# A gated mix of two sequence layers on one core: one load moved to another queue, three groups of work reordered

## The chip, the core and the metric

The kernel runs on one core of a Trainium2 chip. That core has a matrix engine (PE, with PEld for its weight loads), a vector engine (DVE), an engine for activations and scaling (ACT), a general engine (POOL) and SyncE (SP), which only issues DMAs here. DMAs are issued from the queues of SP, ACT and POOL. Every engine works through its own instruction list in order; engines wait for one another by semaphores. The metric is the device time of one execution in microseconds (us), lower is better; "ns" marks nanoseconds.

## The reference

The inputs are x, k and v (2048 x 1024, bfloat16), a diagonal state-space layer A (1024 complex states, matrices B and C, step sizes, a skip vector) and a long convolution B (a 4-tap shift kernel, an ssm kernel of length 2048 per channel, a skip vector).

```python
g = sigmoid((x * gate_w).sum(-1, keepdims=True))
# A: h[t] = Lam_bar * h[t-1] + B_bar x[t];  y = 2 Re(C h) + x * Dskip
a = A_ref(x, Lambda_re, Lambda_im, B_re, B_im, C_re, C_im, log_dt, Dskip)
# B: kv = (4-tap shift of k) * v;  y = fft-convolution of kv with ssm_k over the sequence, + kv * ssm_D;  x * y
b = B_ref(x, k, v, shift_k, ssm_k, ssm_D)
out = g * a + (1 - g) * b
```

## The kernel before

The kernel is one long program in which the order on every engine is written out by hand: the helper `put` chains each instruction behind the one before it on its engine, so PE, DVE, ACT, POOL and SP do their work in the order in which the code emits it. Nearly every instruction therefore has line 94 in the profile, and the tiles tell them apart.

**Opening (lines 147 to 353 and 1022 to 1063).** ACT's queue loads the small parameters: `B_shift_k` (into `skr`), `gate_w` (into `gwr`), then three rows of state parameters (`prow`), and later `B_ssm_D` (`sD`). SP's queue loads the first chunk of 128 channels: two halves of k by DMA transpose (`kT0`), the first half of v between them (`v0`), the ssm kernel by transpose (`kn`), then v's second half. PE starts with dummy products (`raise_clock`), makes columns out of the parameter rows with small products into the PSUM tile `psp` (`columns` does the later ones), and runs the 4-tap sums (`taps`) for both halves. DVE multiplies each half of the taps by v (`ks`). `state_params` (the generator `sp`) has small steps on ACT and DVE: `dtv`, then `abv` on DVE and `rv` on ACT, then more. `fold_K` folds the ssm kernel with ten products into two PSUM tiles (`foldk`), which ACT copies out (`eok`); `mirror` and two DVE sums do the same for v; `fwd_K` and `fwd_V` are the transforms (`psk`, `psv`).

**Convolution loop (lines 1075 to 1195).** For the eight chunks of channels: forward transforms on PE, the complex products of the two spectra on DVE (`products`, tiles G, BT, wkh, t), the inverse transform on PE (`inverse`, PSUM `psz`, copied by ACT to `cv` and stored by SP). Products with x for layer A (`Bu`, PSUM `odd`, `even`, `both`) fill PE in between, with the tiles in `order`, numbered 0 to 15.

**Passage (lines 1197 to 1292).** The last chunk's products and the tiles `Bu(6)`, `Bu(7)`, and the first half of `Bu(8)`. From tile 4 on, the tiles are finished by `turn_U`: ACT scales U's odd half into Q, and POOL adds Q to U's even half by an accumulating DMA, twice, one step after the other; the second addition waits until the first has landed. The 2 by 8 tiles of C are turned by the parameters in `turn_C` (`turning[0]` to `turning[7]`): ACT scales into `m` (or `Q` for pairs 4 and 5), then ACT or DVE scales C itself, and the sum is made by POOL's accumulating DMAs (pairs 0, 1, 4, 5) or on DVE (pairs 2, 3, 6, 7). Tile `u4` has three buffers: U6, the Q of tile 6, and U7 take them, and U8 takes the one that tile 6's Q gives back. PSUM has four buffers for everything.

**Scan loop (lines 1369 to 1419).** Sixteen steps j: DVE scans one state tile (`scan`), `turning` and `turn_U` of later tiles run where the step says so, and `plan[j]` names the products of PE: B8 is tile 8, C0 is the first row block of the output's product with C (PSUM `psy`), G10 a group. `on_act` holds steps of `turn_C` that ACT takes one by one between the copies of `Bu_next` (`filler`). After the loop the last four blocks are finished and stored.

Of the kernel before, what the change touches and what calls it, by code (L numbers as in the profile page):

```python
# [11 lines left out]
BF16 = mybir.dt.bfloat16  # L12
# [8 lines left out]
def kernel(  # L21
# [26 lines left out]
    nc = tc.nc  # L48
    xf = A_x.flatten_outer_dims()
    kf = B_k.flatten_outer_dims()  # L50
    vf = B_v.flatten_outer_dims()
    of = out.flatten_outer_dims()
    S, D = xf.shape
    P = A_Lambda_re.shape[0]
    KS = B_shift_k.shape[1]
    assert S == 2048 and D == 1024 and P == 1024, (S, D, P)
    ND = D // 128
    NP = P // 128
    NT = S // 128
# [6 lines left out]
    PAD = 16  # L66
# [13 lines left out]
    s5p = {"wu": pool("wu", 3)}  # L80
# [11 lines left out]
    def put(eng, f, *a, **kw):  # L92
        with tc.issue_after(prev[eng]) if eng in prev else nullcontext():
            i = f(*a, **kw)  # L94
        prev[eng] = getattr(i, "ins", i)

    def mm(o, l, r, first, last):
        put("pe", nc.tensor.matmul, o, lhsT=l, rhs=r, start=first, stop=last)
# [15 lines left out]
    def copy(o, a):  # L114
        put("dve", V.tensor_copy, o, a)
# [7 lines left out]
    def move(o, i):  # L123
        put("sp", nc.sync.dma_start, out=o, in_=i)
# [17 lines left out]
    ld = pool("ld", 3, side="right")  # L142
# [11 lines left out]
    gwr = rows_[32:32 + ND, 128 * KS:128 * KS + 128]  # L154
    prow = rows_[64:64 + 3 * ND, 0:128]

    nc.scalar.dma_start(out=skr, in_=B_shift_k.rearrange("(j p) k -> j p k", p=128))
    nc.scalar.dma_start(out=gwr, in_=gate_w.rearrange("(j p) -> j p", p=128))
    for i, ap in enumerate((A_log_dt, A_Lambda_re, A_Lambda_im)):
        nc.scalar.dma_start(out=prow[i * ND:(i + 1) * ND, :], in_=ap.rearrange("(j p) -> j p", p=128))  # L160
    pih = consts.tile([128, 1], F32, name="pih")
# [3 lines left out]

    one = consts.tile([128, 1], F32, name="one")
    put("act", nc.scalar.activation, out=one, in_=pih, func=ACT.Sin)
    nc.scalar.dma_start(out=sD, in_=B_ssm_D.rearrange("(o d) -> o d", o=1))

    lds = {}  # L170

# [3 lines left out]
    def load(which, c, held=False):  # L175
        cc = slice(c * 128, (c + 1) * 128)
        if which == "kn":

            t = ld.tile([128, NT, 128], BF16, name="kn", tag="ld")
            if held:  # L180
                hold(t[:, 0, 0:1])
            load_t(t, B_ssm_k[cc, :])
        elif which == "v":

            w = 2 if c == 2 else 1
            if c == NC - 1:
                t = ld.tile([128, NT, 128], BF16, name="v", tag="ld")
            elif c == 2:
                lds["v2"] = xt_pool.tile([128, NT, 2, 128], BF16, name="v2", tag="xT")
            if c < 2:  # L190
                t = ld.tile([128, NT, 128], BF16, name="v", tag="ld")
            elif c < NC - 1:
                t = lds["v2"][:, :, c % 2:c % 2 + w].rearrange("p n k d -> p n (k d)")
            if held:
                hold(t[:, 0, 0:1])
            move(t, vf.rearrange("(n p) d -> p n d", p=128)[:, :, c * 128:(c + w) * 128])
            for k in range(w):
                lds["v", c + k] = t[:, :, k * 128:(k + 1) * 128]
            return
        else:  # L200

            t = ld.tile([128, PAD + S], BF16, name="kT", tag="ld")
            put("pool", nc.gpsimd.memset, t[:, 0:PAD], 0.0)
            if held:
                hold(t[:, PAD:PAD + 1])
            load_t(t[:, PAD:], kf[:, cc])
            if c >= 3:
                lds["kB", c] = ld.tile([128, PAD + S], BF16, name="kB", tag="ld")
        lds[which, c] = t
# [8 lines left out]
        move(a[hi, 10:], a[lo, 8:n - 2])  # L218


    kT0 = ld.tile([128, PAD + S], BF16, name="kT", tag="ld")
    v0 = ld.tile([128, NT, 128], BF16, name="v", tag="ld")
    put("pool", nc.gpsimd.memset, kT0[:, 0:PAD], 0.0)
    for h in range(2):
        hs, ns = slice(h * S // 2, (h + 1) * S // 2), slice(h * NT // 2, (h + 1) * NT // 2)
        load_t(kT0[:, PAD + hs.start:PAD + hs.stop], kf[hs, 0:128])
        if h == 1:
            load("kn", 0)
        move(v0[:, ns], vf.rearrange("(n p) d -> p n d", p=128)[:, ns, 0:128])
    lds["kT", 0], lds["v", 0] = kT0, v0  # L230

    BT = [bt_pool.tile([128, 2, ND, 256], BF16, name=f"BT{g}") for g in range(NG)]
# [52 lines left out]
    ident = consts.tile([128, 128], BF16, name="ident")  # L285
# [3 lines left out]
    def raise_clock(n):  # L289
        for _ in range(n):  # L290
            mm(raised[:, 0], zeros[:, 0:128], zeros, True, True)
# [13 lines left out]
    gwb = consts.tile([128, ND], BF16, name="gwb")  # L305
    pcol2 = consts.tile([128, 4, ND], F32, name="pcol2")
    ident2 = consts.tile([128, 64], BF16, name="ident2")
    psp = ps2([128, 2, 512], "p")
# [7 lines left out]
    dg0 = ks_pool.tile([128, KS, 128], BF16, name="dg", bufs=1)  # L316
    for k in range(KS):
        ts(dg0[:, k], ident, pcol[:, 3 + k, 0:1], None, ALU.mult)
    raise_clock(2)
    mm(psp[:, 1, KS * ND:(KS + 1) * ND], gwr, ident[32:32 + ND, 32:32 + ND], True, True)  # L320
    raise_clock(1)

    def columns():
        mm(psp[:, 0, 0:3 * ND], prow, ident[64:64 + 3 * ND, 64:64 + 3 * ND], True, True)
        copy(pcol[:, 0:3], psp[:, 0, 0:3 * ND].rearrange("p (i j) -> p i j", j=ND))
        copy(gwb, psp[:, 1, KS * ND:(KS + 1) * ND])
        yield
        for q in range(4):
            for t in range(2):
                mm(psp[t * 64:t * 64 + 64, 1, 64 + q * ND:64 + (q + 1) * ND],  # L330
                   skr[:, q // 2 * 64:q // 2 * 64 + 64, q % 2 + 2 * t], ident[32:32 + ND, 32:32 + ND], True, True)
        copy(pcol2, psp[:, 1, 64:64 + 4 * ND].rearrange("p (i j) -> p i j", j=ND))
        tt(ident2, ident[:, 0:64], ident[:, 64:128], ALU.add)

# [464 lines left out]
    turns_U = {}  # L799
# [210 lines left out]
    def step(gen):  # L1010
        next(gen, None)

    def run(gen):
        for _ in gen:
            pass

    def steps(gen, n):
        for _ in range(n):
            step(gen)
# [11 lines left out]
    sp = state_params()  # L1031
# [2 lines left out]
    inverse_cols()  # L1034
    ts(NCF, CF, -1.0, None, ALU.mult)
    step(first)
    step(sp)
    angles = inverse_angles()
    turns = inverse_table()
    run(columns)  # L1040
    run(fold_K(0))
    step(angles)
    run(first)
    dg1 = dgs(1, True)
# [30 lines left out]
    for c in range(NC - 1):  # L1075
        n, nn = c + 1, c + 2
# [157 lines left out]
    with tc.tile_pool(name="fin", bufs=1, side="right") as fin:  # L1234

        count = iter(range(16))

        def room(shape, dt, name):
            return fin.tile(shape, dt, name=name, tag=f"fin{next(count)}")

        prod, back = products(c, 0, room, False), inverse(c - 1)
        run(old)
        steps(prod, 3)
        run(next(tiles))
        steps(turning[0], 2)
        step(back)
        steps(turning[1], 2)
        run(back)
        gate(1)
        gate(2)  # L1250
        steps(prod, 2)
        b6, b7 = Bu(6)
        run(b6)
        run(b7)
        run(turning[0])
        s5p["Q"] = s5p["wu"]
        step(turns_U[6])
        run(turning[1])
        run(prod)
        run(turns_U[6])  # L1260
        b8, b9 = Bu(7)
        run(b8)
        run(b9)
        load_xT(3)
        b10, b11 = Bu(8)
        run(b10)
    back = inverse(c)
    step(back)
    run(back)
    steps(turning[2], 2)  # L1270
    h3.close()
    wk = pool("wk", 5)
    s5p["hb"] = pool("hb", 7)
# [18 lines left out]
    on_act = []  # L1292
# [77 lines left out]
    for j in range(NS):  # L1370
        for k in loaded.get(j, ()):
            loads(k)
        if j == 7:
            store(3)
        for k in stored.get(j, ()):
            store(k)
        advance(j)
        for t in turning[2 * j:2 * j + 2]:
            run(t)
        if j == 0:  # L1380
            run(turning[2])
        on_act += [lambda t=t: step(t) for t in turning[max(3, 2 * j + 2):2 * j + 4] for _ in range(2)]
        turn = turns_U[turned[j]] if j in turned else none
        if j != 10 and plan[j][0:1] != "G":
            step(turn)
        by_group = plan[j][0:1] == "G" and j != 10
        if j == 7:
            scale_b(6)
        if by_group:
            for n, k in enumerate(scaled_b.get(j, ())):  # L1390
                if n == 1:
                    step(turn)
                scale_b(k)
            run(turn)
        if j == 4:
            put_off[-1][0]()
            scale_b(3)
        for unit in plan[j].split():
            if unit == "C0":
                scale_b(2)  # L1400
            if unit[0] == "G":
                Cy_group(int(unit[1]), int(unit[2]))
            else:
                (Bu_next if unit[0] == "B" else Cy_row)(int(unit[1:]), *([[b11]] if unit == "B8" else []))
        if put_off and j not in (4, 12):
            put_off[-1][0]()
        if j == 10:
            step(turn)
            for k in scaled_b[j]:
                scale_b(k)  # L1410
            run(turn)
        elif not by_group:
            run(turn)
            if j == 5:
                run(turns_U[5])
            for k in scaled_b.get(j, ()):
                scale_b(k)
        if j == 7:
            gate(3)
# [48 lines left out]
```

## Time and profile before

| | |
|---|---|
| median of 3 runs | 388.67 us (388.26 to 390.49) |
| the profiled execution: time, span in the trace | 389.03 us, 387.3 us |
| busy in the span: PE, DVE, ACT, POOL | 97%, 96%, 76%, 20% |
| mean DMA rate | 183 GB/s |

A row of a timeline has the start and the length in us, then engine, line, operation, output tile <- input tiles, shapes and a count; in brackets stands how long the engine was idle just before and what released it. In the chain of work that ended last a row is a start, a length and what the chain ran through; "issue" there is time in which the engine waited for nothing that the profile shows. "SPq", "ACTq" and "POOLq" are DMA issues. A row of the view by stretches has, for each engine, its busy us and its number of instructions, then the granted PE clock (1.00 is full), the busy share of the core's DMA engines and their rate. A row of a DMA issue ends with the bytes of one and the median us from issue to landing.

### The profile page before, as it was taken

How to read it: one execution, taken by the hardware profiler on the slowest of the kernel's cores; microseconds unless marked ns; L12 is line 12 of the kernel's file. 1: busy time of each engine (PE TensorE's matmuls, PEld its weight loads, DVE VectorE, ACT ScalarE, POOL GpSimd, SP SyncE). 2: the span in 40 equal slices, each digit the busy share in tenths (PEclk: the TensorE clock that was granted, in tenths of full speed). 3: DMA queues.
4: the chain of work that ended last, by engine and by line, in shares of the span. 5: the costliest groups of instructions: out<-in, count | busy, mean ns of one | idle time of the engine just before them, and what ended most of it. 6: DMA issues, size and time to landing. Idle time of an engine off the chain costs nothing.

```text
span 387.3 us, 6616 instructions
## 1 busy us (share of the span) xinstructions
PE 376.0 (97%) x2445; PEld 196.8 (51%) x2445; DVE 371.5 (96%) x602; ACT 293.8 (76%) x448; POOL 77.5 (20%) x101
## 2 busy tenths in 40 slices
PE   8899899999999999999999899999999999999995
PEld 5466347565484756754454344444444444444442
DVE  8789999999999999999999969999999999999996
ACT  5799997988979789774769398985998859947601
POOL 4011030110301102030004000323323333635100
PEclk9999999999999999999999999999999999999999
DMA  8959999999999998967698989995899999898902
GB/s 158 171 113 234 193 214 191 220 218 155 218 207 215 212 192 173 182 146 137 121 209 174 176 188 213 212 202 102 150 212 212 198 244 239 147 251 160 235 3 108
DMA packets 135506, 70.72 MB, mean 183 GB/s; under 512 B 114921, under 2 KB 117745, under 8 KB 135474
## 3 DMA queue, kind: packets, MB, share of 16 engines
q1 hardware_dynamic: 122992, 46.16, 56.1%
q0 software_dynamic: 12400, 24.12, 37.3%
q8 instruction: 19, 0.31, 0.3%
q14 instruction: 13, 0.11, 0.1%
q10 hardware_dynamic: 82, 0.02, 0.0%
HBM read 12.86 MB, written 8.39 MB: 55 GB/s over the span
## 4 chain that ended last, share of the span: by engine, by line
PE 59%; DVE 20%; ACT 7%; DMA 6%; issue 4%; SPq 2%; DVEq 0%; ACTq 0%
PE psy L94 29%; PE psk L94 7%; DVE BT L94 5%; PE both L94 5%; DVE wkh L94 4%; PE psz L94 4%; PE psv L94 3%; PE even L94 3%; PE taps L94 3%; PE odd L94 3%; DVE G L94 2%; PE foldk L94 2%; SPq L94 2%; DMA U<-Q 2%; DMA CT<-Q 1%
## 5 line engine op out<-in xcount | busy, mean ns | idle before, releaser
L94 PEld LDWEIGHTS <-BT 128*128 128x128 bf16 x640 | 61.7, 98 | 50.5 <-issue 1.7
L94 PE MATMUL both<-xT,BT 128*128 128x512 bf16 x384 | 84.0, 379 | 1.8 <-ACT U L94 1.4
L94 PEld LDWEIGHTS <-hb 128*128 128x128 bf16 x256 | 25.0, 98 | 30.9 <-issue 1.1
L94 PEld LDWEIGHTS <-U 128*128 128x128 bf16 x240 | 23.5, 98 | 28.3
L94 PE MATMUL psy<-CT,hb 128*128 128x512 bf16 x160 | 36.8, 379 | 0.0
L94 ACT ACTIVATE Vh<-psv 128x1024 bf16<-128x1024 f32 x32 | 30.8, 1035 | 7.7 <-PE psv L94 7.6
L94 POOL DMA_DIRECT2D U<-Q x22 | 23.3, 1072 | 62.8 <-ACT Q L94 25.4
L94 PE MATMUL psy<-CT,U 128*128 128x512 bf16 x152 | 34.8, 379 | 0.0
L94 ACT ACTIVATE U<-both 128x512 bf16<-128x512 f32 x44 | 24.2, 594 | 13.9 <-PE both L94 13.7
L94 DVE TENSOR_TENSOR_SCAN W<-rv,init,A 128x256 bf16<-128x256 f32 x48 | 32.1, 729 | 0.0
L94 POOL DMA_DIRECT2D G<-wkh x8 | 9.7, 1218 | 102.8 <-DVE wkh L94 102.8
L94 PE MATMUL psk<-eok,SF 128*128 128x512 bf16 (+1 forms) x120 | 28.1, 354 | 0.0
L94 PEld LDWEIGHTS <-SF 128*128 128x128 bf16 x184 | 18.0, 98 | 19.8 <-issue 1.3
L94 ACT ACTIVATE Q<-U,lam 128x512 bf16<-128x512 bf16 (+1 forms) x44 | 25.5, 606 | 1.1 <-DMA CT<-Q 1.1
L94 PE MATMUL psz<-G,CI 128*128 128x512 bf16 x64 | 24.3, 380 | 1.3 <-DVE G L94 1.3
L94 PE MATMUL psz<-G,SI 128*128 128x512 bf16 x64 | 24.3, 379 | 0.0
L94 PE MATMUL psy<-CTa,hb 128*128 128x512 bf16 x96 | 22.7, 379 | 0.6 <-ACT U L94 0.6
L94 PE MATMUL taps<-dg,kT 128*128 128x128 bf16 (+1 forms) x352 | 21.7, 209 | 0.4 <-DMA kT<-in_B_k_dram 0.4
L94 DVE TENSOR_TENSOR wkh<-BT,Vh 128x3072 bf16<-128x3072 bf16 (+4 forms) x20 | 21.8, 1109 | 0.0
L94 PEld LDWEIGHTS <-kT 128*128 128x128 bf16 x352 | 21.2, 100 | 1.2 <-DMA kT<-in_B_k_dram 0.5
L94 DVE TENSOR_TENSOR wkh<-Kh,Vh 128x3072 bf16<-128x3072 bf16 (+2 forms) x16 | 21.3, 1349 | 0.0
L94 PE MATMUL psk<-eok,CF 128*128 128x512 bf16 x64 | 19.3, 379 | 1.3 <-ACT eok L94 1.3
(221 smaller groups left out, 841.8 us busy)
## 6 DMA issues: line engine op xcount, KB each, us to landing
U<-Q POOLq DMA_DIRECT2D x22, 256.0 KB, 5.2
G<-wkh POOLq DMA_DIRECT2D x6, 768.0 KB, 8.7
cv_scr<-cv SPq DMA_DIRECT2D x16, 256.0 KB, 4.1
v<-in_B_v_dram SPq DMA_DIRECT2D x5, 512.0 KB, 5.7
out_dram<-m SPq DMA_DIRECT2D x8, 256.0 KB, 6.7
BT<-cv_scr SPq DMA_DIRECT2D x7, 256.0 KB, 5.9
out_dram<-BT SPq DMA_DIRECT2D x7, 256.0 KB, 3.5
ks<-lo POOLq DMA_DIRECT2D x6, 256.0 KB, 8.3
```

The costliest lines, as they stand in the source:

```text
L94: i = f(*a, **kw)
```

## The change

Four things move; no product, sum or byte is added or removed.

1. v's first chunk goes from SP's queue to ACT's queue: its first half right behind `B_shift_k`, its second half behind the activation `one`. SP's queue then has k, k, `kn` back to back.
2. `gate_w`'s load goes to the end of ACT's opening loads, its product on PE from the dummy products into the second step of `columns`, and its copy (`gwb`) with it. That second step of `columns` now comes ahead of `fold_K(0)` as before, but the step of `state_params` with `abv` and `rv` comes behind `fold_K(0)`.
3. In the passage, both steps of `turn_U` for tile 6 come ahead of the second parts of `turning[0]` and `turning[1]`.
4. `turning[2]` (C's third tile) is no longer half done before the scan loop and finished in step 0; it is handed to `on_act` in step 0 and finished in step 1, together with `turning[3]`.

```diff
     nc.scalar.dma_start(out=skr, in_=B_shift_k.rearrange("(j p) k -> j p k", p=128))
-    nc.scalar.dma_start(out=gwr, in_=gate_w.rearrange("(j p) -> j p", p=128))
+    kT0 = ld.tile([128, PAD + S], BF16, name="kT", tag="ld")
+    v0 = ld.tile([128, NT, 128], BF16, name="v", tag="ld")
+
+    def load_v0(h):
+        ns = slice(h * NT // 2, (h + 1) * NT // 2)
+        nc.scalar.dma_start(out=v0[:, ns], in_=vf.rearrange("(n p) d -> p n d", p=128)[:, ns, 0:128])
+
+    load_v0(0)
     for i, ap in enumerate((A_log_dt, A_Lambda_re, A_Lambda_im)):
...
     put("act", nc.scalar.activation, out=one, in_=pih, func=ACT.Sin)
+    load_v0(1)
     nc.scalar.dma_start(out=sD, in_=B_ssm_D.rearrange("(o d) -> o d", o=1))
+    nc.scalar.dma_start(out=gwr, in_=gate_w.rearrange("(j p) -> j p", p=128))
...
     for h in range(2):
-        hs, ns = slice(h * S // 2, (h + 1) * S // 2), slice(h * NT // 2, (h + 1) * NT // 2)
+        hs = slice(h * S // 2, (h + 1) * S // 2)
         load_t(kT0[:, PAD + hs.start:PAD + hs.stop], kf[hs, 0:128])
-        if h == 1:
-            load("kn", 0)
-        move(v0[:, ns], vf.rearrange("(n p) d -> p n d", p=128)[:, ns, 0:128])
+    load("kn", 0)
...
-    raise_clock(2)
-    mm(psp[:, 1, KS * ND:(KS + 1) * ND], gwr, ident[32:32 + ND, 32:32 + ND], True, True)
-    raise_clock(1)
+    raise_clock(3)
 
     def columns():
         mm(psp[:, 0, 0:3 * ND], prow, ident[64:64 + 3 * ND, 64:64 + 3 * ND], True, True)
         copy(pcol[:, 0:3], psp[:, 0, 0:3 * ND].rearrange("p (i j) -> p i j", j=ND))
-        copy(gwb, psp[:, 1, KS * ND:(KS + 1) * ND])
         yield
+        mm(psp[:, 1, KS * ND:(KS + 1) * ND], gwr, ident[32:32 + ND, 32:32 + ND], True, True)
         for q in range(4):
...
+        copy(gwb, psp[:, 1, KS * ND:(KS + 1) * ND])
         copy(pcol2, psp[:, 1, 64:64 + 4 * ND].rearrange("p (i j) -> p i j", j=ND))
...
     step(first)
-    step(sp)
     angles = inverse_angles()
     turns = inverse_table()
     run(columns)
     run(fold_K(0))
+    step(sp)
     step(angles)
...
         run(b6)
         run(b7)
+        s5p["Q"] = s5p["wu"]
+        run(turns_U[6])
         run(turning[0])
-        s5p["Q"] = s5p["wu"]
-        step(turns_U[6])
         run(turning[1])
         run(prod)
-        run(turns_U[6])
...
     run(back)
-    steps(turning[2], 2)
     h3.close()
...
         for t in turning[2 * j:2 * j + 2]:
             run(t)
-        if j == 0:
-            run(turning[2])
-        on_act += [lambda t=t: step(t) for t in turning[max(3, 2 * j + 2):2 * j + 4] for _ in range(2)]
+        on_act += [lambda t=t: step(t) for t in turning[2 * j + 2:2 * j + 4] for _ in range(2)]
```

More of the change, by code (lines that the diff above doesn't have):

```diff
@@ L218, in spread @@
         move(a[hi, 10:], a[lo, 8:n - 2])
-    kT0 = ld.tile([128, PAD + S], BF16, name="kT", tag="ld")
-    v0 = ld.tile([128, NT, 128], BF16, name="v", tag="ld")
     put("pool", nc.gpsimd.memset, kT0[:, 0:PAD], 0.0)
     for h in range(2):
-        hs, ns = slice(h * S // 2, (h + 1) * S // 2), slice(h * NT // 2, (h + 1) * NT // 2)
+        hs = slice(h * S // 2, (h + 1) * S // 2)
         load_t(kT0[:, PAD + hs.start:PAD + hs.stop], kf[hs, 0:128])
-        if h == 1:
-            load("kn", 0)
-        move(v0[:, ns], vf.rearrange("(n p) d -> p n d", p=128)[:, ns, 0:128])
+    load("kn", 0)
     lds["kT", 0], lds["v", 0] = kT0, v0
```

## The prediction

> **What bounds the kernel now.** I read the view by stretches first, cut where the chain of work changes engine.
>
> ```profile
> 0.00:47.04 47.04, 42.48 (x342) 24.80 (x343) 41.60 (x87) 37.34 (x45) 6.67 (x19) 1.00 0.95 172
> 47.04:138.26 91.22, 91.22 (x765) 56.08 (x766) 90.44 (x81) 77.05 (x125) 12.37 (x16) 1.00 1.08 204
> 190.70:222.24 31.54, 29.74 (x194) 13.99 (x193) 31.30 (x37) 20.71 (x39) 5.14 (x6) 1.00 1.00 184
> 222.24:257.53 35.29, 34.70 (x161) 15.68 (x161) 31.89 (x67) 32.18 (x51) 7.94 (x9) 1.00 1.01 206
> 257.53:383.00 125.47, 125.42 (x608) 57.05 (x607) 122.97 (x275) 87.47 (x134) 39.24 (x45) 1.00 0.86 175
> ```
>
> After 47.04 PE (first engine column) is never idle except in two stretches of the passage, by 1.80 us (1.44 in one piece, below; the rest waits for DVE's own pace and stays) and 0.59 us, and DVE (third) is nearly as full. The granted clock is 1.00 throughout. So time can come from three places only: the opening, which delays everything behind it, and the two holes of PE. What is saved there reaches the end only if DVE, nearly as full, comes forward by as much. Next I read the chain of work that ended last, for the opening and the passage.
>
> ```profile
> 7.00 3.74 DMA v<-in_B_v_dram
> 10.83 1.23 DVE ks L94
> 12.06 0.09 DVE abv L94
> 12.17 0.21 ACT rv L94
> 12.38 1.83 ACT eok L94 x2
> 14.26 2.97 PE psk L94 x15
> ...
> 204.80 2.08 ACT CTa L94 x2
> ...
> 213.34 7.49 DMA U<-Q
> ...
> 223.30 2.87 issue
> ...
> 228.39 0.61 DVE trn L94
> ...
> 237.37 0.81 DVE CT L94 x2
> ...
> 249.11 5.78 DMA CT<-Q
> ```
>
> The opening hangs on v's second half: its landing (10.74), then `ks`, then `abv` and `rv`, and only then may ACT, in its order, copy the folded kernel (`eok`) that PE waits for. The passage hangs on the second addition to U6, on a hole of 2.87 us in DVE, and on the additions to C's fifth tile (CT<-Q). The timelines of the passage show the three holes with their releasers:
>
> ```profile
> 206.78 1.32 ACT L94 ACTIVATE Q<-U,lam 128x512 bf16<-128x512 bf16 x2
> 208.39 0.86 POOL L94 DMA_DIRECT2D U<-Q  x1 [0.37 <-ACT Q L94]
> 220.85 0.22 ACT L94 ACTIVATE U<-ends 128x4 bf16<-128x4 bf16 x1 [6.63 <-DMA U<-Q]
> 222.24 34.69 PE L94 MATMUL both<-xT,BT 128*128 128x512 bf16 x160 [1.44 <-ACT U L94]
> 223.88 2.20 ACT L94 ACTIVATE m<-CTa,mc2i 128x1024 bf16<-128x1024 bf16 x2
> 232.09 0.21 ACT L94 ACTIVATE U<-ends 128x4 bf16<-128x4 bf16 x1
> 254.91 1.34 ACT L94 ACTIVATE Q<-U,lam 128x512 bf16<-128x512 bf16 x2 [1.12 <-DMA CT<-Q]
> 257.53 2.75 PE L94 MATMUL psy<-CTa,hb 128*128 128x512 bf16 x12 [0.59 <-ACT U L94]
> ```
>
> ACT sits until 220.85 because U8's buffer is still being read by U6's second addition. Four PSUM tiles fill up, and PE stops at 220.80 for 1.44 us. DVE stops from 223.30 until ACT has read C's third tile (223.88 + 2.20 = 226.08). PE stops again before 257.53, since ACT waited for CT<-Q.
>
> **The change part by part.** Parts 1 and 2 belong together.
>
> ```profile
> 1.34 0.28 ACTq L158 DMA_DIRECT2D rows<-in_gate_w_dram  x1
> 2.06 0.56 SPq L94 DMA_DIRECT2D v<-in_B_v_dram  x1
> 4.07 0.23 ACTq L168 DMA_DIRECT2D rows<-in_B_ssm_D_dram  x1
> 4.54 2.41 SPq L94 DMA_TRANSPOSE kn<-in_B_ssm_k_dram  x1
> 9.12 0.42 DVE L94 TENSOR_SCALAR NCF<-CF 128x1024 bf16<-128x1024 bf16 x1
> 9.63 0.39 PE L94 MATMUL foldk<-kn,ident 128*128 128x512 bf16 x1
> 11.73 0.22 PE L94 MATMUL foldk<-rows,refl 1*128 1x128 bf16 x1
> 13.99 1.22 DVE L94 TENSOR_TENSOR ks<-ks,mirror 128x1024 bf16<-128x1024 bf16 x1
> ...
> v<-in_B_v_dram SPq DMA_DIRECT2D x2, 256.0 KB, 3.9
> v<-in_B_v_dram SPq DMA_DIRECT2D x5, 512.0 KB, 5.7
> DMA to landing us min/median/max: 4.6/4.6/4.6
> 4.00:8.00 4.00, 3.55 (x47) 3.16 (x47) 3.93 (x8) 2.47 (x4) 0.40 (x1) 1.00 1.08 203
> ```
>
> (The row with 4.6 is that of the `kn` tile.) v's second half is issued on ACT's queue where `B_ssm_D` was, some 0.28 later because v's first half (0.56) took the place of `gate_w` (0.28): 4.35. With the chain's 3.74 it lands at 8.1; DVE is free for the second `ks` only at 9.12 + 0.42 = 9.54, so sharing of the DMA engines may cost it 1.4 us unseen. `ks` then starts at 9.54 instead of 10.83. But this no longer sets `eok`: with `abv` and `rv` behind the fold, ACT waits for `foldk` alone, and that for `kn`. In the changed kernel's instruction order the issue of `kn` carries a wait for v's first half: 1.34 + 3.9 = 5.24, against 4.54 before. Plus 4.6, `kn` lands at 9.84. The DMA engines are busy at 1.08 from 4 to 8 us, and the same bytes were all in by 10.74 before, so `kn`, now the last, lands between 9.84 and 10.74; I take 10.2, a little nearer the former because the first half of v and the second of k start about 0.7 earlier. From the first fold product to the end of the last are 11.95 - 9.63 = 2.32; one copy is 1.83/2 = 0.92, with 0.1 of handovers: PE goes on at 10.2 + 3.34 = 13.54 instead of 14.26, a gain of 0.7. Bounds: if `kn` lands as early as 4.54 + 4.6 = 9.14, the gain is 1.8; if v's first half takes the 5.7 of the row of 512 KB, `kn` is issued at 7.04, lands at 11.64, and 0.7 is lost.
>
> DVE's mirror sums of v ended at 15.21 before, 3.26 behind the fold's last product; now at 12.52 + 3.26 = 15.8, while psv, at 14.26 + 2.97 = 17.23 before, needs them at 16.5: covered. The rest of these parts costs nothing that shows: `gate_w`'s product, its copy and the eight small products stand ahead of the fold on PE, while PE waits for `kn`; ACT's queue issues two DMAs more before the next activation, which waits for DVE until 6.01 (below); POOL's queue and the parameter rows are not held. If `gate_w`, last in ACT's queue, landed behind `kn`, it would hold the fold in its place.
>
> ```profile
> 6.01 1.06 ACT L94 ACTIVATE SF<-rq 128x1024 bf16<-128x1024 f32 x1 [1.32 <-DVE rq L94]
> ```
>
> [...]
>
> **Part 3.** Q's two ACT instructions now start where the scaling of C stood, 2.08 earlier (chain: 204.80 to 206.78), so the first addition is issued near 206.3 instead of 208.39. It landed in at most 4.95 (208.39 to 213.34, when the second one went out), so the second goes out near 211.3 and lands, at 5 to the 7.49 of before, at 216.3 to 218.8. ACT then needs about 1.2 for U8's first copies, and a PSUM tile is free by 220.0, before PE needs it at 220.80: the hole of 1.44 goes. Behind the waiting second addition POOL's queue now holds the four additions to C's first tiles; they go out near 212 to 216. Waiting for them are `m` of pairs 2 and 3 on ACT, which takes their buffers, and the first output block at 255; the first `m` comes some 6 us after they went out, behind U8's copies, both `cv`, Q and U8's other half, and the same additions landed within 4.95 or so beside this traffic: covered. If the second addition took 9.3 or more, the hole would return.
>
> **Part 4.** DVE no longer waits for C's third tile, and its three instructions on that tile move behind the next scan with the same length: DVE gains the 2.87. In step 1 DVE comes to C's fourth tile (all counted without the opening's gain, which moves everything) at 223.3 + 8.98 (a scan, 228.39 to 237.37) + 2.22 (C's third tile, 226.17 to 228.39) = 234.5. ACT has to have made pair 3's `m` by then; it did the same list, from U8's first copy to the end of tile 7's Q, in 11.2 us (220.85 to 232.09), and started at 218.8 ends it at 230.0: 4.5 us of room. Everything on DVE up to C's fifth tile comes 2.8 earlier (0.07 left for handovers), so CT<-Q goes out at 246.3 and the chain from there to PE (257.53 - 249.11 = 8.42) ends at 254.7. PE, 1.44 earlier, is there at 255.5: the hole of 0.59 goes too. Parts 3 and 4 need one another: without the second, PE's 1.44 would be given back at 257.5. Middle: 1.44 + 0.59 = 2.03; bounds 2.03 and, where C0 starts as before, 0; it goes below only by the fourth rival. After that PE runs to the end, and the last scan still feeds it, since DVE is 0.8 further ahead than PE:
>
> ```profile
> 375.12 0.49 DVE L94 TENSOR_TENSOR hb<-hb,trn 128x256 bf16<-128x256 bf16 x2
> 375.88 3.62 PE L94 MATMUL psy<-CT,hb 128*128 128x512 bf16 x16
> ```
>
> **Sum.** 0.7 + 1.44 + 0.59 = 2.7 us. The profiled execution took 389.03 (span 387.3), so 386.3 of it; it is 0.36 above the median of the runs, 388.67, from which I forecast 385.9.
>
> **The rivals.** First: the opening gains nothing. v's second half and `kn` share the engines, and `kn`, now last, lands when v did, at 10.74; PE then goes on at 14.08, and 0.2 is left. Against it speaks only that the queues start earlier. Time: 388.67 - 2.03 - 0.2 = 386.4; chance 0.20.
>
> Second: v's first half lands late and holds `kn` at its queue, as in the lower bound: 0.7 lost, 2.03 gained, 387.3; chance 0.10. It is worse than the first only if that half takes over 4.8.
>
> Third: the middle is not cashed. DVE does not come forward by more than a little (the wait for C's third tile becomes one for pair 3's `m` or for the second addition to U7), CT<-Q stays near 249, and PE stands longer before 257.5. Only the opening is left: 388.0; chance 0.11. Against it speaks the room of 4.5 us for pair 3's `m`.
>
> Fourth, slower: the additions to C's first tiles, held on POOL's queue, land so late that `m` of pairs 2 and 3, which waits for their buffers on ACT, comes late, and DVE stands in step 1. PE's margin at C0 is 255.5 - 254.7 = 0.8, so every us past 234.5 + 0.8 = 235.3 is a us of PE, and the kernel is slower than before from 235.3 + 2.7 = 238.0 on; at 240.1 it takes 390.7. The additions would have to land some 20 us after they went out, where the slowest of the chain took 7.49. Chance 0.09.
>
> **How the numbers follow.** The forecast, with kn between 9.6 and 10.6 and the middle whole, has 0.50, and 385.3 to 386.3 as its own range. Half a per cent, which is what a measurement of this kernel can tell from no change, is 1.94 us, so faster means below 386.73. That holds the forecast, most of the first rival (0.13 of its 0.20) and nothing of the others: 0.63. Slower is the fourth alone, 0.09; the rest is 0.28. The range goes from the upper bound of the opening with the whole middle, 388.67 - 1.8 - 2.03 = 384.8, to the third rival with a little over, 388.3.
>
> **What would show it.** The second `ks` starts near 9.5 and no longer waits for v. The first `foldk` starts near 10.2, the first row of psk with both folds near 13.5, and the first `psz` near 46.3 instead of 47.04. U8's first copy on ACT starts by 219; PE has no row with 1.44 idle, nor one before the first `psy`, which starts near 254.8. DVE has no hole of 2.87 between the first two scans. Wrong would be: `foldk` after 10.8; a new wait of DVE in front of C's third or fourth tile; a wait of ACT for CTa<-m; or PE idle again before the first `psy`, which would say that the chain through CT<-Q did not move.

## The result and the profile after

The changed kernel takes 387.87 us (median of 22 runs, 385.73 to 391.56) where the kernel before takes 389.51 (22 runs, 387.37 to 392.75). The ratio is 0.996, with a 95% interval of 0.994 to 0.9979: faster by 0.4%, some 1.6 us, where 2.7 were forecast. The profiled execution says more: 385.94 us with a span of 384.2, against 389.03 and 387.3. That is 3.1 less, so the gain of the profile and the gain of the medians have to be brought together.

First the timeline of the opening after the change:

```profile
0.75 2.59 SPq L94 DMA_TRANSPOSE kT<-in_B_k_dram  x2
1.34 0.43 ACTq L163 DMA_DIRECT2D v<-in_B_v_dram  x1
5.54 2.09 SPq L94 DMA_TRANSPOSE kn<-in_B_ssm_k_dram  x1
5.69 1.96 PE L94 MATMUL taps<-dg,kT 128*128 128x128 bf16 x32 [1.33 <-DMA kT<-in_B_k_dram]
10.03 0.39 PE L94 MATMUL foldk<-kn,ident 128*128 128x512 bf16 x1
10.05 1.21 DVE L94 TENSOR_TENSOR ks<-taps,v 128x1024 bf16<-128x1024 f32 x1
13.46 0.38 PE L94 MATMUL psk<-eok,CF 128*128 128x512 bf16 x1 [0.36 <-ACT eok L94]
46.25 0.39 PE L94 MATMUL psz<-G,CI 128*128 128x512 bf16 x1 [1.30 <-DVE G L94]
```

The fold starts at 10.03 (forecast 10.2), psk with both folds at 13.46 (13.54), psz at 46.25 (46.3). One row was not foreseen: the first taps wait for k until 5.69, with PE idle for 1.33, where they started at 4.38 before. Then the passage:

```profile
209.39 0.86 POOL L94 DMA_DIRECT2D U<-Q  x1 [2.88 <-ACT CTa L94]
210.14 3.64 POOL L94 DMA_DIRECT2D CTa<-m  x4
213.66 0.22 ACT L94 ACTIVATE U<-ends 128x4 bf16<-128x4 bf16 x1
216.42 38.15 PE L94 MATMUL both<-xT,BT 128*128 128x512 bf16 x172
245.39 3.63 POOL L94 DMA_DIRECT2D CT<-Q  x4 [5.94 <-DVE CT L94]
254.40 2.75 PE L94 MATMUL psy<-CTa,hb 128*128 128x512 bf16 x12
```

U8's first copy no longer waits (213.66 for 220.85). PE runs from 216.42 to the first psy without a hole, and that starts at 254.40 for 257.53. The view by stretches shows the same for DVE, the third engine column, busy for 32.60 of 33.12:

```profile
0.00:46.25 46.25, 41.63 (x339) 24.25 (x343) 41.63 (x87) 37.47 (x45) 6.22 (x19) 1.00 0.95 173
221.45:254.57 33.12, 32.96 (x152) 15.01 (x154) 32.60 (x70) 29.04 (x48) 7.08 (x8) 1.00 1.06 222
```

So in this execution nearly every time came as forecast. One cause did not: by the forecast the fold starts when `kn` lands, and in the chain of work that ended last it starts when PE has done its own work behind the late k. The last row below is from the DMA issues:

```profile
0.75 4.90 DMA kT<-in_B_k_dram
...
10.10 2.27 PE foldk L94 x10
...
kn<-in_B_ssm_k_dram SPq DMA_TRANSPOSE x2, 4.2
```

`kn`, issued at 5.54, was in near 9.7, while PE was busy with the taps and small products until 10.03. So it is luck that 10.03 is close to 10.2. This execution is also the second fastest of its 22 runs.

### The profile page after: what moved, and what is told of

Read it like the earlier page. It is cut to its first block, busy times and chain, and to the rows that moved or that the text cites. A ratio compares the mean times of both kernels' runs of the same rounds, so it can differ in the third digit from the quotient of the medians.

```text
span 384.2 us, 6583 instructions
## 1 busy us (share of the span) xinstructions
PE 373.1 (97%) x2411; PEld 196.2 (51%) x2445; DVE 371.7 (97%) x602; ACT 294.3 (77%) x448; POOL 77.1 (20%) x101
## 4 chain that ended last, share of the span: by engine, by line
PE 75%; DVE 14%; ACT 4%; issue 3%; DMA 3%; SPq 1%; DVEq 0%
PE psy L94 29%; PE both L94 17%; PE psk L94 7%; DVE BT L94 5%; PE psz L94 5%; PE taps L94 4%; DVE wkh L94 4%; PE even L94 3%; PE psv L94 3%; PE foldk L94 3%; PE odd L94 3%; DVE G L94 2%; ACT Vh L94 1%; DMA BT<-in_A_B_im_dram 1%; DMA kT<-in_B_k_dram 1%
## 5 line engine op out<-in xcount | busy, mean ns | idle before, releaser
L94 PE MATMUL psy<-CTa,U 128*128 128x512 bf16 x87 | 20.4, 379 | 0.1
```

## The experiments

Between psk and the first psz, and between the first psy and the end, every profile of this study takes the same time within 0.4 us. An execution is therefore told by two numbers: when the first psz starts (the opening), and how long it is from there to the first psy (the passage). All profiles, in us, each worked out from those two rows; the last column is when PE came to its full rate, explained under the next experiment:

| kernel | first psz | psz to psy | span | full rate from |
|---|---|---|---|---|
| before | 47.04 | 210.49 | 387.3 | 5.28 |
| before, again | 47.59 | 209.84 | 387.2 | 7.88 |
| changed | 46.25 | 208.15 | 384.2 | 4.28 |
| changed, again | 48.35 | 208.84 | 386.9 | 10.47 |
| parts 1 and 2 | 47.61 | 208.49 | 386.2 | 8.68 |
| parts 3 and 4 | 47.16 | 208.15 | 385.0 | 6.54 |
| part 3 | 46.97 | 208.40 | 385.1 | 6.06 |
| part 4 | 46.97 | 208.90 | 385.6 | 6.22 |
| changed, v behind the rows | 46.96 | 208.15 | 384.8 | 6.42 |
| the same, gate_w second | 48.77 | 208.15 | 386.7 | 5.89 |
| changed, six dummy products | 46.68 | 208.15 | 384.6 | 6.62 |
| parts 1 to 3, six dummies | 46.22 | 208.16 | 384.1 | 5.35 |
| parts 1 and 2, six dummies | 46.12 | 210.16 | 386.0 | 4.45 |
| before, three dummies fewer | 47.44 | 212.98 | 390.2 | 9.66 |

**The change again.** No edit.

> The changed kernel once more, beside the three below. The runs so far have 389.51 before and 387.87 after, a gain of 1.6 us, while the two profiled executions are 3.1 apart (spans 387.3 and 384.2). If the profiled gain is what the change does and the medians scatter by chance, this run comes to about 386.4 to 386.9 against 389.5 for the kernel before. If about half of it is lost in most executions, it comes to 387.9 again, and the profile of this run should show where: the first foldk later than 10.03 and the first psz later than 46.25 (the opening loses it), or PE idle again between 215 and 255, with the first psy later than 254.4 (the passage loses it).

387.24 us against 388.22 for the kernel before, ratio 0.9968 (0.9953 to 0.9982). The passage is nearly the same, the opening is 2.1 later. Its timeline:

```profile
5.54 3.60 PE L94 MATMUL taps<-dg,kT 128*128 128x128 bf16 x32 [1.18 <-DMA kT<-in_B_k_dram]
9.20 2.55 PE L94 MATMUL taps<-dg,kT 128*128 128x128 bf16 x32
12.13 0.39 PE L94 MATMUL foldk<-kn,ident 128*128 128x512 bf16 x1
15.56 0.38 PE L94 MATMUL psk<-eok,CF 128*128 128x512 bf16 x1 [0.36 <-ACT eok L94]
```

The same 32 products start as early and take 3.60 instead of 1.96. The view by stretches, PE alone (stretch, length, PE's busy time and products, granted clock, DMA share and rate), first of the fast profile of the change, then of this one:

```profile
6.00:6.50 0.50, 0.50 (x13) 1.00 1.33 239
8.50:9.00 0.50, 0.50 (x13) 1.00 1.27 289
```

```profile
6.00:6.50 0.50, 0.50 (x8) 1.00 1.34 226
9.50:10.00 0.50, 0.50 (x7) 1.00 0.00 0
10.50:11.00 0.50, 0.50 (x12) 1.00 0.00 0
```

PE is busy all the time in both. A row counts every product that is under way in its stretch, some of them in two rows, so 13 and 8 understate the difference: in the trace the products start 56 ns apart in the one and 107 ns apart in the other, until 10.47. The granted clock reads 1.00 in every row, but the view puts 1.00 where the trace has no entry. The trace's record of that clock begins at 4.28 in the first of these executions and at 10.47 in the second, and in every profile in which products run at that moment it begins where 107 ns (427 for a product of 512 columns) give way to the shorter distance (56, and 216 for 512 columns). The last column of the table is where the record begins.

**The two halves of the change.** `opening_alone` applies parts 1 and 2 to the kernel before, `passage_alone` parts 3 and 4.

> Parts 1 and 2 alone. Additive theory: the opening gives the 0.8 of the profiled executions (psk 13.46 for 14.26, psz 46.25 for 47.04) and nothing takes it back: 0.8 less than the kernel before, 0.998. Rival, the opening gains nothing in most executions, because the first half of k now lands later (5.65 for 4.09) and its landing scatters: 0 to 0.4 more than before. The margin theory: PE gains 0.8, but DVE's pace and the hole of 1.44 in the passage grow by what was gained, so that psy starts where it did: 0.

> Parts 3 and 4 alone. Additive theory: the holes of 1.44 and 0.59 go, 2.0 to 2.3 us less than the kernel before (0.994 to 0.995), the first psz at 47.04 as before, the first psy near 255.2, no hole of 2.87 on DVE. If the medians lose half of the gain in the passage, it is about 1.0 less than before, and its profile has PE idle before psy or a later landing of CT<-Q. If the opening is what loses it, this kernel is as fast as the whole change, within 0.3.

Parts 1 and 2: 389.03 us, ratio 1.0012 (0.9998 to 1.0027), no gain. Parts 3 and 4: 386.82 us, 0.9959 (0.9944 to 0.9974), the whole gain of the change or a little more. The opening is what loses it. Its profile without the rest has the slow start again, full rate from 8.68 on:

```profile
5.60 3.41 PE L94 MATMUL taps<-dg,kT 128*128 128x128 bf16 x32 [1.23 <-DMA kT<-in_B_k_dram]
14.82 0.38 PE L94 MATMUL psk<-eok,CF 128*128 128x512 bf16 x1 [0.36 <-ACT eok L94]
```

The runs say so too. With the passage of the change in both, they lie from 386.53 to 386.86 with the opening of before (5 runs), and from 385.76 to 388.72 with the new one (12 runs).

**What delays k, and whether the gap starts the slow stretch.** `v_behind_rows` issues v's first half after the parameter rows; `more_dummy_products` leaves the loads alone and fills PE's gap.

```diff
-    load_v0(0)
     for i, ap in enumerate((A_log_dt, A_Lambda_re, A_Lambda_im)):
         nc.scalar.dma_start(out=prow[i * ND:(i + 1) * ND, :], in_=ap.rearrange("(j p) -> j p", p=128))
+    load_v0(0)
```

> The whole change, but v's first half issued behind the three parameter rows on ACT's queue, some 1.4 us later, and so kn, which in the instruction order then waits for the first of these rows instead of v's first half, about 1.5 us earlier. If v's first half is what makes the first half of k land at 5.65 instead of 4.09, it lands near 4.2 to 4.6 again, taps start by 4.7, the fold starts at 8.7 to 9.3 and psk near 12.2 to 12.8: up to 1 us less than the whole change. If instead the two transposes of k issued back to back share the engines, k lands near 5.6 here too, taps stay at 5.7, the fold stays near 10.0 behind PE's own work, and the time is that of the whole change within 0.3. If v's first half comes too late for the first ks at 8.23, DVE waits there, and psv rather than psk moves.

```diff
-    raise_clock(3)
+    raise_clock(6)
 
     def columns():
```

> The whole change, with six dummy products in front of the taps instead of three, so that PE is not idle from 4.36 to 5.69 while it waits for k. Theory of the slow start: PE's products run at half their rate (8 of the taps in 0.5 us instead of 13) until PE has been busy without a gap for some time, and the gap that the change put in front of the taps starts this anew in most executions (full rate from 9.2 and 10.2 in the two profiles that lost, already at 5.7 in the one that won). Then the taps run at full rate from 8 us at the latest, the second psk starts between 13.4 and 14.7, the time is 0.5 to 1.3 less than that of the whole change (about 0.993 of the kernel before), and the runs lie closer together. Rival, the spread comes from the landing of k and kn: the three products change nothing, 0.997 and the same spread.

The first: 386.59 us, 0.9954 (0.9939 to 0.997), runs from 386.32 to 386.84. Its timeline and a row of its chain of work that ended last:

```profile
4.17 3.03 PE L94 MATMUL taps<-dg,kT 128*128 128x128 bf16 x32
10.74 0.39 PE L94 MATMUL foldk<-kn,ident 128*128 128x512 bf16 x1
14.17 0.38 PE L94 MATMUL psk<-eok,CF 128*128 128x512 bf16 x1 [0.36 <-ACT eok L94]
...
5.30 4.95 DMA rows<-in_gate_w_dram
```

The taps start at 4.17 although both transposes of k still go out together: it was v's first half, issued at 1.34, that held k back. PE's gap is gone, and with it the spread. What was won is then lost at `gate_w`, which lands at 10.25, last in its queue.

The second: 386.09 us, 0.9938 (0.9924 to 0.9952), runs from 385.77 to 386.56. Three idle-filling products and nothing else:

```profile
2.90 2.74 PE L94 MATMUL raised<-wkh 128*128 128x512 bf16 x6
5.69 2.38 PE L94 MATMUL taps<-dg,kT 128*128 128x128 bf16 x32
13.89 0.38 PE L94 MATMUL psk<-eok,CF 128*128 128x512 bf16 x1 [0.36 <-ACT eok L94]
```

k lands as late as in the whole change (the taps start at 5.69 in both), yet, with the full rate from 6.62, the kernel gains some 1.2 us over it (0.9938 for 0.9968, of 388.4, from two sets of runs), and its runs lie within 0.8. The rival of late landings falls; this version beats both kernels.

From 107 ns a product to 56 the products start 1.9 times as fast, and where the record of the granted clock shows changes, the stretches from its start to the first change and from change to change are whole multiples of 3.41 us, or nearer 3.413: 6.83, 3.41 and 368.64 (2, 1 and 108 of them) in the profile with gate_w second, below, and 378.88 (111), from 4.28 to 383.16, in the first profile of the change. What begins or ends such a stretch is not shown.

PE starts at 1.19 in every profile. In the ten that have no gap of note in front of the taps, or a gap only after the full rate (0.43, parts 1 and 2 with six dummies), the full rate comes between 4.45 and 7.88. In the four with a gap of 0.9 to 1.3 in all, it comes at 8.68, 9.66 and 10.47, and once at 4.28, just before the gap; that is the fast profile of the change, and there the idle time of 1.33 did not take it away again. So it differs from execution to execution whether the gap costs anything. How much idle time puts the full rate off is not shown.

**The reverse: take the dummies from the kernel before.**

```diff
-    raise_clock(2)
     mm(psp[:, 1, KS * ND:(KS + 1) * ND], gwr, ident[32:32 + ND, 32:32 + ND], True, True)
-    raise_clock(1)
```

> The kernel before without the three dummy products between the first small products and the taps, so that PE is idle there for 1.2 in all, as it is in the changed kernel. Theory of the slow start: PE comes to its full rate later than 7.8 us in most executions, the first taps take 3.4 and more instead of 2.4 to 2.8, the fold starts 0.5 to 2 later, the time is 0.3 to 1.5 more than before (1.001 to 1.004) and the runs spread wider. Rival: the dummies do nothing, 1.000.

389.36 us, 1.0032 (1.0018 to 1.0045), runs from 388.56 up to 391.95. Slower, as the theory has it, and the taps are slow until 9.66, in the second half:

```profile
4.01 3.60 PE L94 MATMUL taps<-dg,kT 128*128 128x128 bf16 x32 [0.20 <-DVE dg L94]
7.66 2.89 PE L94 MATMUL taps<-dg,kT 128*128 128x128 bf16 x32
```

The profile itself does not carry the whole difference: its psz is only 0.4 later than in the first profile of the kernel before, and most of its longer span lies in the passage (212.98, 2.5 more). There the granted clock is at one half from 197.39 to 200.81, behind 64 products of one column and an idle time of 0.42:

```profile
194.59 1.74 PE L94 MATMUL p<-gwb,xT 128*128 128x1 bf16 x64
197.50:198.00 0.50, 0.50 (x3) 0.50 1.28 287
```

3.41 us at half the rate are some 1.7 of the 2.5. No other profile has this fall, and whether the dummies have a part in it is not shown.

**The opening with the dummies, alone.** Parts 1 and 2 with `raise_clock(6)`.

> Parts 1 and 2 alone, with six dummy products in front of the taps instead of three. Theory of the slow start: the opening is then worth what the prediction gave it, 0.7, as far as PE is at its full rate by 8 us: 0.4 to 0.8 less than the kernel before (0.998 to 0.999), where parts 1 and 2 without the dummies gave 1.0012. Rival: the opening gains nothing because kn or v lands late, and this kernel is at 1.000 to 1.001 like the one without them.

387.8 us, 0.9992 (0.9974 to 1.001): inconclusive, as the interval holds both theories. The profile explains why: psz starts at 46.12, 0.92 earlier than in the first profile of the kernel before, but the passage of before takes 210.16, and PE waits there for U8's buffer again:

```profile
219.65 0.22 ACT L94 ACTIVATE U<-ends 128x4 bf16<-128x4 bf16 x1 [6.82 <-DMA U<-Q]
221.04 34.69 PE L94 MATMUL both<-xT,BT 128*128 128x512 bf16 x157 [1.13 <-ACT U L94]
```

**gate_w early.** A try to keep the taps at 4.2 and start the fold at 9.6: v behind the rows, `gate_w` second in the queue.

> As with v behind the rows, and gate_w second in ACT's queue again, where the kernel before had it. With v behind the rows the taps started at 4.17 and the fold could have started near 9.6, but PE stood idle to 10.2 and the fold began at 10.74, behind the small product of gate_w, whose row came in at 10.25 as the last of the queue. Theory: without that wait the fold starts at 9.6 to 9.8, psk's second row at 13.0 to 13.3 instead of 14.17, and the time is 0.8 to 1.1 less than with v behind the rows, 0.993 of the kernel before. Rival: kn's landing holds the fold just as long, and the time is the same within 0.3.

388.56 us, 0.9991 (0.9971 to 1.0012), from 386.5 to 390.4. A miss. Its chain and its timeline:

```profile
3.74 7.78 DMA kn<-in_B_ssm_k_dram
...
11.57 0.39 PE L94 MATMUL foldk<-kn,ident 128*128 128x512 bf16 x1 [2.06 <-DMA kn<-in_B_ssm_k_dram]
13.76 0.63 PE L94 MATMUL foldk<-kn,refl 128*128 128x512 bf16 x1
```

`kn`, issued at 3.74 beside both halves of v, takes 7.78 to land, where it took 4.6 before. And PE, idle for 2.06, falls back to the slow rate some time later: a product of the fold takes 0.63 instead of 0.38. This time the granted clock shows it, at one half from 12.72 to 16.14:

```profile
12.50:13.00 0.50, 0.50 (x3) 0.72 0.04 8
13.00:13.50 0.50, 0.50 (x3) 0.50 0.00 0
```

More than half of the executions seem to have it. In seven of the twelve runs the mean granted clock is 0.993 to 0.995 and the time 388.4 to 390.4; in the other five it is 0.997 to 1.000 and 386.5 to 387.8.

**The parts of the passage.** Part 3 alone, then part 4 alone.

> Part 3 alone: both steps of tile 6 ahead of C's. By the prediction, the hole of 1.44 goes, but DVE's hole of 2.87 stays, CT<-Q goes out near 249 as before, and PE gives the 1.44 back before the first psy: no gain, 0.998 to 1.001. Rival: DVE is not what sets the first psy, and the 1.44 is kept: 0.996, the whole of what parts 3 and 4 measure together.

> Part 4 alone: C's third tile a scan later. PE's hole behind U8 stays, DVE no longer stands for 2.87, CT<-Q goes out earlier and the 0.59 before psy goes: 0.59 less, 0.998 to 0.999. If the second part of tile 6's sum then lands later because C's additions crowd it, the hole grows and nothing is gained. Rival: the two parts do not need one another and this one holds the whole gain: 0.996.

Part 3: 386.84 us, 0.9958 (0.9945 to 0.9971), as much as parts 3 and 4 together. Part 4: 387.52 us, 0.9975 (0.9965 to 0.9984). Part 3's timeline, then part 4's:

```profile
218.26 2.18 ACT L94 ACTIVATE m<-CTa,mc2i 128x1024 bf16<-128x1024 bf16 x2
223.17 0.48 DVE L94 TENSOR_SCALAR CTa<-CTa,c2r 128x1024 bf16<-128x1024 bf16 x1
246.10 3.63 POOL L94 DMA_DIRECT2D CT<-Q  x4 [2.79 <-DVE CT L94]
```

```profile
219.95 0.22 ACT L94 ACTIVATE U<-ends 128x4 bf16<-128x4 bf16 x1 [6.21 <-DMA U<-Q]
221.34 34.69 PE L94 MATMUL both<-xT,BT 128*128 128x512 bf16 x157 [0.59 <-ACT U L94]
246.27 3.63 POOL L94 DMA_DIRECT2D CT<-Q  x4 [2.72 <-DVE CT L94]
```

With part 3 alone ACT reads C's third tile at 218.26 instead of 223.88, so DVE finds it ready at 223.17 without a hole, and CT<-Q goes out at 246.10 for 249.11. DVE's 2.87 and PE's 1.44 had one cause, the wait for U8's buffer. Part 4 alone gains some 1.0 us (0.9975 of 388.6) where 0.59 was expected: it too takes away DVE's hole and PE's wait before the first psy, by moving the tile. That part 4 is not needed beside part 3 follows from the whole without it as well:

> Parts 1 to 3 with the six dummy products, part 4 left out. The prediction said that parts 3 and 4 need one another: then this is 2.0 slower than the whole change with the dummies, near 0.999. The profile of part 3 alone says that ACT, no longer held at U8's buffer, comes to C's third tile early enough by itself: then it is as fast as the whole change with the dummies, 0.9938, within 0.3 us.

386.03 us, 0.9944 (0.993 to 0.9958), and 384.1 in its profile: part 4 adds nothing beside part 3.

**The kernel before again.** No edit.

> The kernel before once more, for its profile. The profile of the prediction had PE idle by 1.44 behind U8 and by 0.59 before psy, where tile 6's second addition landed 7.49 after its issue; in the profiles with parts 1 and 2 alone, or part 4 alone, it landed after some 6.2 to 6.4 and PE's hole there was 0 and 0.59. If this landing scatters, this profile has another hole than 1.44 and another span by as much; if it is fixed by the order of the kernel before, the hole is 1.4 again.

388.93 us, span 387.2, and another passage:

```profile
4.38 3.62 PE L94 MATMUL taps<-dg,kT 128*128 128x128 bf16 x32
220.59 0.22 ACT L94 ACTIVATE U<-ends 128x4 bf16<-128x4 bf16 x1 [5.71 <-DMA U<-Q]
218.36 38.31 PE L94 MATMUL both<-xT,BT 128*128 128x512 bf16 x172
225.92 0.49 DVE L94 TENSOR_SCALAR CTa<-CTa,c2r 128x1024 bf16<-128x1024 bf16 x1 [1.44 <-issue]
```

The hole of 1.44 behind U8 is not there (PE waits 0.51 at 214.91 and 0.76 before the first psy), and DVE's is 1.44 instead of 2.87. This opening was later by 0.55 (taps slow to the end, 3.62), so PE came later and waited less. The holes of before are no fixed price.

## Why the prediction was right and wrong

**Direction right, size too large.** Forecast -2.7, measured -1.6 (ratio 0.996). The median after, 387.87, is 2.0 above the forecast 385.9: 1.1 of that is the smaller gain, and 0.8 the base, as three runs of the kernel before gave 388.67 and 22 gave 389.51.

**The opening, 0.7: this term failed.** The prediction made the fold wait for `kn` alone and took k, and PE's taps behind it, as unmoved. `kn` came as it said or better: held at its queue until v's first half was in, issued at 5.54 (forecast 5.24), landed near 9.7 (10.2). But v's first half, now issued at 1.34, delays k's first half, and the taps start 1.3 later (5.69 for 4.38). At PE's full rate they and the small products end at 10.03, so that 0.8 was still gained in the first profile. PE, out of dummy products, stands still in front of them for 1.18 to 1.33, though, and where its full rate had not come before this gap, it came at 8.68 and 10.47: in two of the three profiles and, by the times, in most executions.

Mean of the first psz: 47.15 over the five profiles with the loads and dummies of before, 47.40 over the three with the new opening, 46.34 over the three with six dummies. So the term is -0.25 as made, and 0.81 once PE is kept busy, near the 0.7. Worked back from the second set of runs, 387.24 is 1.30 above the profiled 385.94: psk near 14.8, with the passage at its shortest. Only 5 of the 34 runs of the change lie below 386.6.

"Wrong would be: foldk after 10.8" came in the typical execution (12.13, 11.39), not in the profiled one. The first rival, that the opening gains nothing, is what came, but not by its cause, a late `kn`. The second rival, 387.3, is nearest in time if the ratio is taken (0.996 of 388.67 is 387.1), with the same wrong cause. The median itself is nearest to the third, 388.0, which has it the other way round: there the opening pays and the middle does not.

**Part 3, 1.44: right in mechanism, read off one execution.** U8's copy went from 220.85 to 213.66, earlier than the 216.3 to 218.8 of the forecast, because the two additions landed 3.7 and at most 4.3 after their issue (205.65, 209.39), not 4.95 and 5 to 7.49. What it is worth depends on what the passage of before costs: 210.49, 209.84, 208.49 and 210.16 in four profiles with the passage of before (the fifth, 212.98, has the fall of the clock in it), against 208.15 to 208.84 with parts 3 and 4. The forecast took the first, the longest of the four. Parts 3 and 4 measure 0.9959, 1.6 us of 388.22, for the 2.03 of the forecast.

**Part 4, and "parts 3 and 4 need one another": wrong.** Part 3 alone holds the whole gain. DVE's hole came from ACT's late start, and the prediction gave it a cause of its own. It did let ACT's list start earlier, at 218.8, in the sum for part 4, but not where it said that without part 4 PE's 1.44 would be given back. That the two holes of PE go was right.

**The fourth rival** (additions held on POOL's queue) did not come: they went out at 210.14, and DVE took C's third tile with no wait.

## What to carry to other kernels

PE's idle time in front of this kernel's first real products (0.9 to 1.3 in four profiles) was paid twice in three of them: once as the wait, and again as a slow stretch, up to 8.68, 9.66 and 10.47; in the fourth the full rate had come before it, at 4.28. When an early load is moved, look at what else lands before those products, and let dummy products reach up to them (0.9938 for 0.9968 here). Before a hole of one profile is booked as a gain, look at it in a second profile; two holes behind one late buffer are one gain, not two.

## What the runs showed of the hardware

Products of 128 columns started 107 ns apart until some time between 4.28 and 10.47 (5.28 in the first profile of the kernel before), and 56 ns apart after it. The trace's record of the granted clock begins at that moment, and the 1.00 that the view shows before it is no reading. Two falls of that clock to one half stand among the products, each for 3.41: at 12.72, after an idle time of 2.06 (the profile with gate_w second), and at 197.39, after 64 products of one column and an idle time of 0.42 (before, three dummies fewer). An idle time of 1.33 at 4.36 brought none in the first profile of the change, where the clock falls at 383.16, behind PE's last product.

The transpose of k's first half landed 4.90 after its issue with a 256 KB load of v issued 0.6 behind it on ACT's queue; with that load behind the rows, the taps that wait for it started 3.4 after its issue. The `kn` transpose took 4.6 to land in the kernel before and 7.78 where both halves of v were issued beside it. U6's second addition (256 KB) landed 7.49 after its issue in the first profile of the kernel before, with C's four additions issued ahead of it, and at most 4.3 after it where it went ahead of them.
